# Five blocks instead of four in two query groups of a fused attention and MLP kernel, with a new instruction order

## The chip, the cores and the metric

The kernel runs on one core of one Trainium2 chip. The metric is the device time of one execution in microseconds, the median of several runs. The core has five engines: TensorE (PE, matmuls into PSUM), VectorE (DVE), ScalarE (ACT), GpSimd (POOL) and SyncE (SP, which issues the DMAs). PSUM has eight banks of 512 fp32 columns. The profile names the engines by their short names, and PEld is the weight load of TensorE.

## The reference

All tensors are bfloat16. `x` has 2048 rows of 640; there are 32 heads of 20 columns.

```python
xn = layernorm(x)
# A: attention
q, k, v = split_heads(xn @ wqkv)            # 32 heads, Dh = 20
p = softmax(q @ k.T * 20 ** -0.5)           # 2048 x 2048 for each head
s = (p @ v).merge_heads() @ wo
# B: a mixer and an MLP
h = gelu(layernorm(xn) @ w1)                # its four quarters are shifted by 1, -1, 2, -2 rows
x1 = xn + shifted(h) @ w2
g = silu(x1 + gelu(layernorm(x1) @ w3) @ w4)  # w3: 640 x 1536, w4: 1536 x 640
return x + s * g
```

Most of the work is the softmax: 32 x 2048 x 2048 exponentials.

## The kernel before

**Tiling.** Four heads make a quad, so there are eight quads (0 to 7), and each quad has four query groups of 512 queries (`qc` 0 to 3). A group is named quad_group below: 3_3 is quad 3's last, 7_1 is quad 7's second. In a group the 2048 keys are 16 key tiles of 128. A score tile is one head, one key tile and 512 queries, and takes one PSUM bank, so a group has 64 score tiles.

**Two ways to the exponential.** On the plain way (`k` in `order`, function `score_act`), TensorE makes the four score tiles of a key tile, ScalarE takes two banks at a time through Exp (L1707: 128x1024) into the buffer `PT`, and four matmuls (L1447) multiply them by V and add into the group's bank `PVB`, which is bank 7. A *wide* key tile (`w`, `score_rows`) has its four scores made in one burst, and one ScalarE instruction of 128x2048 takes all four banks (L1684).

The other way is a *block* (`b`, functions `score_both` and `block_bits`): two key tiles, eight score tiles. Four of them go to ScalarE as above (two instructions at L1707). The other four are made on VectorE: each is scaled and written as uint16 (L1729, 128x512, the names `u...`), which makes the bits of a bfloat16 power of two. To lower the error this is done with four offsets: the bits themselves, and three copies with a constant added (the "pieces" `s..._1` to `s..._3`). Each of the four versions is multiplied by V (L1629, four matmuls each). So the VectorE half of a block costs sixteen matmuls where the plain way has four.

Blocks go through `block_bits` in units of one or two. The pieces of a unit of two blocks are 4096 wide, those of a single block 2048. A piece is made on VectorE (L1617) unless the set `PP` names it by the number of the unit's first block and the offset; then GpSimd makes it (L1615, as int32). Outside group 0_0, `PP` names pieces 2 and 3 of the unit that starts with block 0 and piece 3 of the unit that starts with block 2.

`ND` says for each group how many blocks it has, and `UNITS[ND]` says after which plain key tiles they come (position, place in the unit, size of the unit):

```python
UNITS[4] = ((0, 0, 2), (1, 1, 2), (3, 0, 2), (5, 1, 2))
UNITS[5] = ((0, 0, 2), (1, 1, 2), (3, 0, 2), (4, 1, 2), (6, 0, 1))
self.BLK = [(2, 3), (6, 7), (10, 11), (14, 15), (0, 1)]
out.append(("r" if i in rows else "w" if 100 + i in rows else "k", ks[i]))   # in order(); i counts the plain key tiles
```

`NR[7][1]` is `(107,)`: in group 7_1 the plain key tile number 7 is wide, if the group has that many. A group with four blocks has eight plain key tiles (0 to 7), one with five has six (0 to 5). `NR[3][3]` is `(112,)`, which no group with four blocks reaches.

**Scores on TensorE.** The score of a head needs 20 of the 128 rows. It is made either as one matmul on 32 rows ("rows", L1638), where the matmuls of several heads that stand behind one another run at the same time on different rows, or as four matmuls of 32 columns on all rows ("columns", L1655), against queries of which only that head's rows are not zero. Which it is follows from the neighbours in TensorE's order.

**The end of a group.** `normalise` reads bank 7 with a transpose on VectorE (L1748), takes the reciprocal of the sums (L1755), multiplies on GpSimd (L1761) and sends the result to memory. The next group's first product with V can only be written after L1748.

**The rest.** All projections (L748) of the attention and of branch B are put between the scores on TensorE. Branch B needs ScalarE for its two Gelus (L2018; L2110, twice two instructions of 128x6144) and a Tanh (L2138), and VectorE for the evictions (L2103, L1314, L1376, L2012, L2046, L2132). During quad 7 the output projection of the finished groups starts, and `last_half` works on group 7_3 in two halves.

**The order.** Every engine works through a fixed list. The lists come from one string, `TABLE`: each entry is two characters for a task's number, then one character for each PSUM bank set or `PT` slot that it takes. `follow` reads it from front to back, `plan_sync` puts in the semaphore waits. So the order on each engine, the bank of every tile and the rows-or-columns choice all come from the string.

Of the kernel before, what the change touches and what calls it, by code (L numbers as in the profile page):

```python
# [490 lines left out]
class Cfg:  # L491
# [5 lines left out]
    def __init__(self, S=2048, D=640, H=32, F=1536):  # L497
# [114 lines left out]
        self.ND[6][1] = 5  # L612

# [58 lines left out]
class Gen:  # L672
# [1481 lines left out]
    r"#9###Z#0#,#%#$#[#]#6#&#:#'#w#(#^$`#)$S#d%p#5#;&R#`$'#l#<#_#=#c#b#>&Q#-#4#?#2#.$K#f#@&S#g#a#A#*#B#h$L#p#C#e#n#D#i#m$J#E#j#q#F$N$M#o#G#k#r#H$O#+#I#s#x$T$U#J$P#K#{"  # L2154
    r"#L#t#M#|#N$V#O#y#P$Q%$$#Q#}#v#R$R#S$X#z#T#u#U#~${&$W$8$|$#%%$}%&%'$q)$)$r$v#$w$x$s$l($m$(%($y$n$o$~#V$Y$$$z$Z$t#W%##X$[#Y$u$p$,$a%n%`($*%a$]$+%b$%%c$^$5&[#%g'$-"
    r"$6%h%i$_$&%d%j$.$9%k$/%8%%.&%e&]$7%/%l%0%1&^%9%))%2%:%;%*%3($2%4%5%f%6&c$%<$0%q&d&e$:%+$@&_$3%7%,%-%=&%>$D&f&j%%?&`$A&g$4&k%@$b&l%C$;%r($C$B$1&m&n&T)%s&U%A&V&W&"
    r"X#7$c&o%B%t&$<%u&Y%v&w%&a$E%m&x$?%o&y&z$>&{$d%w$F*@%&|%E*;'*<&*?$$G%x&h*=%'(%')$='*&6$$e'+$f%D$I&7*A#',*9'$g*8&'-$h&8*:)&9&}%$H&:*5%*4$$i&;$j*+&*6'**'&~(H%y'#'$"
# [136 lines left out]
```

## Time and profile before

| | |
|---|---|
| median of 3 runs | 779.2 us (778.91 to 779.86) |
| the profiled execution | 780.64 us, its span 778.9 us |
| granted TensorE clock | 0.997 |
| TensorE, ScalarE, VectorE, GpSimd busy | 767.8, 761.1, 701.4, 441.3 us |

Where the stages of the change lie is read from the transposes at L1748, one at the end of each group: group 3_3 runs from 371.6 to 404.4 us and group 7_1 from 698.5 to 720.8 us. Group 3_3 is longer than the others (20 to 24 us), because two of the Gelu instructions at L2110 stand in it.

A line of a group view reads: line, engine, operation, output <- input with shapes, xcount | busy us, mean ns of one | idle us of the engine just before them, and what ended it. Busy time counts overlapped instructions once, so the busy time divided by the count is less than the mean duration where instructions overlap. A line of the windows view gives, for a stretch of time, the busy us of each engine and in brackets how many instructions started in it.

### The profile page before, as it was taken

What the parts mean: (1) busy time and instruction counts of PE and PEld (TensorE: products, weight loads), DVE (VectorE), ACT (ScalarE), POOL (GpSimd) and SP (SyncE); (2) the same over time, 40 slices, a digit from 0 to 9 for tenths busy, and PEclk for the clock granted to TensorE, in tenths of its full rate; (3) what the DMA queues carried; (4) which work ended last, traced back from release to release, by engine and by line L of the source; (5) the groups of instructions that cost most, each with busy time, mean ns of one, the idle gap of its engine ahead of it and who ended that gap; (6) DMA issues with size and microseconds to landing.
All of it is one profiled execution on the core that took longest, in us unless ns stands there. A gap on an engine that the chain in (4) does not pass through costs nothing.

```text
span 778.9 us, 28219 instructions
## 1 busy us (share of the span) xinstructions
PE 767.8 (99%) x12594; PEld 296.5 (38%) x12594; DVE 701.4 (90%) x1177; ACT 761.1 (98%) x802; POOL 441.3 (57%) x238
## 2 busy tenths in 40 slices
PE   8999999999999999999999999999999999999996
PEld 4433333334444333233534334333334333333454
DVE  8889899988999999998988889999998899997786
ACT  7999999999999999999999999999999999999995
POOL 6386745564547657566464664766553635635742
PEclk9999999999999999999999999999999999999998
DMA  5315343364112423433343232324431023114443
GB/s 173 51 57 116 97 85 77 63 163 77 20 39 46 77 64 81 81 66 75 59 115 57 24 71 56 74 58 87 111 52 33 9 54 93 21 19 109 129 142 104
DMA packets 141353, 58.13 MB, mean 75 GB/s; under 512 B 113728, under 2 KB 136432, under 8 KB 141232
## 3 DMA queue, kind: packets, MB, share of 16 engines
q1 hardware_dynamic: 141232, 56.33, 32.8%
q8 instruction: 99, 1.62, 0.9%
q14 instruction: 22, 0.18, 0.1%
HBM read 34.70 MB, written 10.33 MB: 58 GB/s over the span
## 4 chain that ended last, share of the span: by engine, by line
PE 55%; ACT 41%; DVE 2%; DMA 1%; SPq 1%; issue 0%
ACT arena L1707 36%; PE psum L748 20%; PE psum L1638 14%; PE psum L1629 9%; PE psum L1447 7%; PE psum L1655 2%; ACT arena L2110 1%; ACT arena L1684 1%; ACT arena L2018 1%; DMA arena<-in_A_wqkv_dram 1%; SPq L935 1%; PE psum L1504 1%; ACT arena L2138 1%; PE psum L1478 1%; PE psum L1508 0%; DVE arena L1729 0%
## 5 line engine op out<-in xcount | busy, mean ns | idle before, releaser
L1707 ACT ACTIVATE arena<-psum 128x1024 bf16<-128x1024 f32 x730 | 675.0, 1075 | 5.8 <-PE psum L1638 3.7
L1615 POOL TENSOR_TENSOR arena<-arena 128x2048 int32<-128x2048 int32 x92 | 330.3, 3600 | 212.9 <-DVE arena L1617 126.3
L1729 DVE TENSOR_SCALAR arena<-psum 128x512 uint16<-128x512 f32 x532 | 342.8, 682 | 30.9 <-PE psum L1638 24.4
L748 PE MATMUL psum<-arena 128*32 128x320 bf16 (+1 forms) x5808 | 335.2, 333 | 0.4 <-ACT arena L1102 0.2
L1638 PE MATMUL psum<-arena 32*128 32x512 bf16 x1872 | 242.7, 384 | 1.4 <-ACT arena L1707 0.6
L1629 PE MATMUL psum<-arena 128*22 128x512 bf16 x2128 | 186.0, 382 | 0.2
L748 PEld LDWEIGHTS psum<-arena 128*32 128x32 bf16 x5808 | 138.2, 96 | 120.8 <-issue 44.2
L1638 PEld LDWEIGHTS psum<-arena 32*128 32x128 bf16 x1872 | 65.3, 91 | 208.9 <-ACT arena L1707 111.5
L1447 PE MATMUL psum<-arena 128*22 128x512 bf16 x1452 | 138.7, 382 | 0.0
L1617 DVE TENSOR_SCALAR arena<-arena 128x4096 uint16<-128x4096 uint16 (+1 forms) x124 | 133.7, 1095 | 1.0 <-PE psum L1629 0.2
L1629 PEld LDWEIGHTS psum<-arena 128*22 128x22 bf16 x2128 | 48.0, 90 | 63.4 <-issue 42.2
L1761 POOL TENSOR_TENSOR arena<-arena 128x512 bf16<-128x512 f32 x30 | 41.5, 1383 | 32.6 <-DVE arena L1617 27.6
L1447 PEld LDWEIGHTS psum<-arena 128*22 128x22 bf16 x1452 | 35.0, 90 | 52.0 <-issue 35.1
L1655 PE MATMUL psum<-arena 128*32 128x512 bf16 x476 | 46.3, 380 | 0.3
L2103 DVE CAST arena<-psum 128x512 bf16<-128x512 f32 x48 | 32.7, 684 | 3.8 <-PE psum L748 3.6
L1314 DVE CAST arena<-psum 128x512 bf16<-128x512 f32 x40 | 27.1, 685 | 4.7 <-PE psum L748 4.3
L1926 POOL TENSOR_TENSOR arena<-arena 128x640 bf16<-128x640 bf16 x12 | 16.8, 1402 | 21.5 <-DVE arena L1860 5.5
L959 DVE BATCH_NORM_STATS2 arena<-arena 128x6 f32<-128x320 bf16 x54 | 24.4, 477 | 1.6 <-DMA arena<-in_A_x_dram 1.6
L1748 DVE STREAM_TRANSPOSE arena<-psum 128x512 f32<-128x512 f32 x30 | 21.3, 711 | 2.5 <-PE psum L1629 1.5
L1860 DVE SCALAR_TENSOR_TENSOR arena<-psum,arena 128x320 bf16<-128x320 f32 x32 | 15.5, 486 | 8.3 <-PE psum L748 8.0
L1684 ACT ACTIVATE arena<-psum 128x2048 bf16<-128x2048 f32 x12 | 22.8, 1900 | 0.0
L2132 DVE TENSOR_TENSOR arena<-psum,arena 128x320 bf16<-128x320 f32 x32 | 15.6, 489 | 7.4 <-PE psum L748 7.2
(135 smaller groups left out, 340.9 us busy)
## 6 DMA issues: line engine op xcount, KB each, us to landing
arena<-in_B_w_dram SPq DMA_DIRECT2D x48, 160.0 KB, 2.7
arena<-arena SPq DMA_DIRECT2D x124, 32.0 KB, 1.9
arena<-in_B_w_dram SPq DMA_DIRECT2D x4, 960.0 KB, 5.5
arena<-in_A_x_dram SPq DMA_DIRECT2D x8, 320.0 KB, 5.5
arena<-in_A_x_dram SPq DMA_DIRECT2D x16, 160.0 KB, 3.0
out_dram<-arena SPq DMA_DIRECT2D x16, 160.0 KB, 2.6
heads<-arena SPq DMA_DIRECT2D x120, 20.0 KB, 2.0
arena<-keys SPq DMA_DIRECT2D x28, 80.0 KB
```

What stands on the lines that cost most here:

```text
L748: ins = e.matmul(pb[32 * c:32 * c + 32, 0:N], lhsT(k, c), rhs(k, c), start=(k == 0), stop=(stop and k == nk - 1), tile_position=(0, 32 * c))
L1447: ins = e.matmul(pb[32 * i:32 * i + 22, 0:512], VA[:, ql, kts[i // 2], i, :], PT[:, slots[i // 2][0].slot, slots[i // 2][0].at(i % 2):slot ...
L1615: return e.tensor_tensor(dst.bitcast(I32), U[:, ub, 0:w].bitcast(I32), bass.AP(c.tensor, c.offset, [list(c.ap[0]), [0, w // 2]]), op=ALU.add)
L1617: fa if onp else lambda e, v=v, dst=dst: e.tensor_scalar(dst, U[:, ub, 0:w], EXP_B[v], None, op0=ALU.add),
L1629: ins = e.matmul(pb[32 * i:32 * i + 22, 0:512], wv, dst[:, at:at + 512].bitcast(BF16), start=first, stop=final, tile_position=(0, 32 * i))
L1638: return e.matmul(out, self.KT[32 * i:32 * i + 32, b, 128 * kt:128 * kt + 128], q, start=True, stop=True, tile_position=(32 * i, 0))
L1655: ins = e.matmul(out[32 * c:32 * c + 32, :], self.KT[:, b, 128 * kt + 32 * c:128 * kt + 32 * c + 32], self.QM[:, gb, i, :], start=True, st ...
L1684: lambda e: e.activation(self.PT[:, hp[0].slot:hp[0].slot + 2, :], self.psum[:, 512 * h0.slot:512 * h0.slot + 2048].rearrange("p (a b) -> ...
L1707: lambda e: e.activation(self.PT[:, hp.slot, :].rearrange("p (a b) -> p a b", b=512), self.banks(hs), AF.Exp, scale=cfg.scale),
L1729: T("dve", c_dve(512), lambda e, h=h, y=y: e.tensor_scalar(U[:, ub, y:y + 512], self.bank(h.slot)[:, :], a_exp, EXP_BIAS, op0=ALU.mult, op ...
L1761: return e.tensor_tensor(OnT.rearrange("p (k d a) -> p a k d", k=4, a=4), Ob[:, :].rearrange("p (a k d) -> p a k d", a=4, k=4), in1, op=AL ...
L2103: T("dve", c_dve(512), lambda e, h=h, fc=fc, i=i, G=G: e.tensor_copy(G[:, i, fc, :], self.wbank(h)[:, 0:512]), reads=[wa], writes=at, name ...
```

## The change

Groups 3_3 and 7_1 get a fifth block: key tiles 0 and 1, which were plain, become the block. It is a unit by itself and comes behind the group's last plain key tile. Because 7_1 has six plain key tiles now, its number 7, the wide one, is gone. No entry of `PP` names a unit that starts with block 4. `TABLE` is replaced as a whole (16,901 characters before, 16,941 after); the new string begins with the same entries with some neighbours exchanged.

```diff
         self.ND = [list(x) for x in self.ND]
         self.ND[6][1] = 5
+        self.ND[3][3] = 5
+        self.ND[7][1] = 5
...
 TABLE = (
-    r"#9###Z#0#,#%#$#[#]#6#&#:#'#w#(#^$`#)$S#d%p#5#;&R#`$'#l#<#_#=#c#b#>&Q#-#4#?#2#.$K#f#@&S#g#a#A#*#B#h$L#p#C#e#n#D#i#m$J#E#j#q#F$N$M#o#G#k#r#H$O#+#I#s#x$T$U#J$P#K#{"
...
+    r"#9###Z#0#,#[#%#6#$#:#]#&#'#^#w#($`#d#)$S%p#;#5#`&R#<#_#=#c#>$'#l#b#-#?#4#2&Q$K#f#@#.&S#g#a#A#*#B(Q#h$L#p#C#n#e#D#i#m$J#E#j#q#F$N$T$M#o#G#k#r#H$O#+#I#s#x$U#J$P#K"
...
```

More of the change, by code (lines that the diff above doesn't have):

```diff
@@ new lines @@
+    r"V&W&X#7&o$c%B$<&Y&w$&x&y&z&{&a#8%t%%m$?%o%u$E$>%v$d%w$F*<#&|%E*@'*?&*;$$G%x&h*=#&6$&7$='((')$e$f'*%D$I'+*A(',*8#$g*9$'-$h&8(H&9&:$H&}(*4&*5'$i*:$&;$j**#*+$*6%&~"
+    r"%y'#'$'%$k*>*,)%Z$%[%F)%G%]%H'&(I%P#%Q%R%U(%V%W%^%X%S%I%z%K'%L%M%N%{&%J%Y%|%T%}%~%_*1&*C'*2%*B(%O&#*D#&&$&$&'&(&)*3'&<&**.(&+'d*-'';''<'=&%'>'?&-&H(*/&&.&I'@&p&"
+    r"2&&J'A&K&3&,&L&0*0*`'&M*_&*J#*K$*I)*H(*a$&?(*N&@&A*M'.&4'*L)&B&N&C''+''+(&&5&D*P(*Q#*O)*E+)&*T*7'/''0&=(*F*S(&q&&r*X&*W'&>*G'1'2*Y''3*[)*Z(*R%'4&s&t*U*]#&u+2&*h"
@@ new lines @@
+    r"$+3'*V&v*i%+4%*k*c(*b)'I&*l'J'K*d('L'M'N+$&+%%*^+T+&)&E*n'*o#*p$*m('5$*r'6'7*q#'8'9+5&*s+6%+*+7'':*e+C'*f#+D(*g$*v'B$(P'C+E)'D'E'F'U('V'G'W*y'X*j&'Y+<'+=&'Z+.(+"
+    r"/)+8+>('O('P+#'Q'R'S']#+:#'T+9$+X&+0''^+;%+[+W%+,)++('_'H+Z'`'a+-&*x*|+K#'b+_&+J$+`%+?+b+o'+H)+G(+1+L#+c&F)+I(*{+r+n#+U$+V%*w&G+Y'&O#,*),+(+q*z-.(J*u,,%&P,.$+v&"
+    r",-#+u%*t+y+M,/&+^'+](*}+x'f$+a('g+A$+@#,J%,K&'e'h+B#'i+|+i(+h''j,L$*~'l''k+F'c'm&i'n+j#+N3$(K+f&+e%,;#,:):V,&'o,>'p+g)+d'q+s(+t',0+w',B#,=,A&,8%,9$+k,D,<%+l)+m("
@@ new lines @@
+    r"'r#,E+O's+p)'t,@#,H&,?$,G%,#'u+P'v,I(,C#'x$'y'w'z'{'|,N%,O&,X('}+},P&,),[,x#,w$'~,W),M,Z05,y',`',Q%,R&,_(+Q,',c(M$,S(,p$,b,q#+z+R,$(N,r)(#,T,t),s(->&-?'+{,u&,e,"
+    r"F(L'[&/,5%+~-@#-1$-#(-2#,~),%-4,(-$$,d,4&-5(%##/(&(O,f,6(,v,1#,](,^),2$('((,3%,i(+((,(-(),a),z$,{#(*(.,l(/,|&,7-%((0-9'-&)-8&,h-'%-<,j(R,V#,U$-H%+S-;,Y(,}-G'-K-"
+    r"0)-/(-(,g-J-3&-M%-O#-L&-N$,o,n,k-P%-j(-R-k)(1#(Y(2-Q&1-l(-6%-7&(3($.`-U,m-:)-A(-F$-B)-E#(4(5-)-I$-X(7)(8(9(6-=-C'(:-*-h$-p#.%'-g%-i&(v(;-s-_.$(06(Z$(<([(a.&$(]-"
@@ new lines @@
+    r"x$-w#-d&-c%-D-z(=(^-e%-+-v'-{-u((_-W-y'-Y(`-}&-[-~%.1#.2$-,-T.##.5-q).('.)(-V-t-m.*)(D-Z-a%.4-`&.'-b(.8).,#.9(.+$(S#.;(T.-#(U.<-o&-n%/9)(V(W-r&/8(..(X-f/:$.=./%"
+    r".7&.6'.0$(@(>(w&.?-].:#(x-|-^(y.3&(z.B.I&-S.J(({.M$.E(?((|(A.H(B.L#)D.>.@.N&.c%.d(.T'.S&(C0I$.f.K(o--(E.U%0J.P#.g.O$.k%0K.n.Q#.D.V'.j(.W&0L.m.X(0M/k%.h$.i#0N.R("
+    r"}.A.l'/n.a(.z'.b).C.}.G)(.e#.y&.q$.p%.Y.F.|07&(F.r&/$).t(.s'/%&.Z08.u%.~$/'/#%09.o/(/&).x(.w)/F'0:/I0;.{(.v/?$0</5&/@%/6'/)/A%/+/40=&0>0?/7)0@/<%/U(/./V)/=$0A/>"
@@ new lines @@
+    r"(0C#.[450B0D0E0F/W'0G/|&/K$/{%/J#/N#0H/-/B(~$0P)#)$/}&)%0O/d$/R'/S(/1/*)&(h/T%/E#/D%/C&/;/H/0/G(/X/Y'/g/Z(/,/[%/j#)'/M&/~$0#%///P(b$0$'(c.]/](/m/^'/L&(d/_$/O/c%"
+    r"/a$/b#(e/f.^(f/e)0%0)'/i&0*((g/h%/`/l'/q/t/Q)/0R$0S0T0+$0U0&$0V0'%/2/34O'0W0X%/w0Y4R0Z0[0]48)49'4E%4F&0^0,$0-#0(4G(4</s/o/r4;4@(0.#4N'4H&4I%/z4Q/u4J&/v4C4>#4=$4"
+    r"U)4V'/y4A'4X0/4S%4T&4?(4Y/p4W%/x4L$4B4M#0_#004P)0`4j&4k%46(47)0a010b0Q4l$4]0c0e'0f4K4:#5##4r&4q%0d4`0g0h5&4s(0i5((4w'5))0j5*&4f4D4z4u&4v%4x#0k(p'4{5s(q4y#5,(4~)"
@@ new lines @@
+    r"5+'(r5%(s5-)(t4c57&56%(u4_5:'52#5/(50'51)5.55)=4b53%5I$59%._5458&5J#4^5K&5<4a4|)4}(4n'5;5H5$))>()?5B4o&4e)@4p'4g$Eg5T)4h#5S()A5?0s5'5U%4Z4[)B5>0n4i)4d)C5a)5M&5L"
+    r"'5b(5E4t)K5d5N#5X%5W$))&5e)*5[()+5Z)5Y(5P&5Q'),5]5R'5O5_%5`$5^)-5=5c&).5w&5u(5v'5t)&b5V025z4m5x#)R6K$5~#6L%5y5F5C6M%5A6%&Z6*'036+(5}&5G6$6,'5@5|)6'%6($5k5f6)$5D"
+    r"5{(5g6I'61#6H&5l5i5m6J)60%(i'645h5j6#((j63(k6/&6.'5n0468#67%6_)6^(62&(l6:6&(m6-6;6b(66%65&6O'6N(n6=69#)E$6P()F)6)G6Q%7H)H6m%6R#6S$6n&0l6>)I6T'6A6G)J0m#0o6@6o$6?"
@@ new lines @@
+    r"0p6X$6g(6f)6Y#6U6[6<6h#)o6W&6V%6])L#)M6Z&5o6j(6`$6i)6a#)N6c)O6D6k%)P6{&6d6|%6e7#))Q6B6u#6w)6t$6v(6l)v6z6y6x'7=')0(7<&)10q)27>%6p)6}$6~#6q(Ef)37%#371)479'7$7:&6C"
+    r"6r&7;)6F)573$76)72#75(6s7()Y77#)7()8)h)97?74&):7+7@&);6E7A$)S&)<7P$7.)T)U)V7Q%7T')W7'78)X7I(7J'7L)7K&7,7M&7O7R#7g$7h%7&7N7B7k#7S)8('8)(7U5p7-7)7V8*(7b&7`$7c#7a%"
+    r"7*7e708?)5q7d%7/7f8>()Z)7C7j'8@)7i#8-$8,%)})[7m)])a80$7W7l7v8/)8%(8&')^828'&7y8<$8.#8;%)_83)818='84(86'8+)`5r7n87%)b&898E%8F$85&)c88)d8G#8e'8d(8f&8K)8A8N)e)f8g%"
@@ new lines @@
+    r"7D8h$)g8L)8B&8:8i)8O8C')i&8~)j7p8D%)k8o$8n%8l)8k()l)m8p()p)7s)q)n8j)r8m$8S'8v$8u#8R%0r)s8V)t8H8I))u8J(8q8w&8M)8U7r8Q#8r&8s'8P$7q8T$)w(7E)x)y7t)z8t(7]$7{(7[#7z)7"
+    r"w8Y7F7oEt)7u){)~#*#)|7|'7^#3%*$*%*(EuEh(8]EiEj*&7xEk9-(9%#9B$9&)*'El8`Ev9E3#0tEn#Eo8_Em7GEpEwEq9)8^8Z90Ex8xEz$9(E{E|ErEyE}9,(9;$9<#9C%*)Es8bE~9?1%)1&11#1'9F121("
+    r"1)13141*3&&3H(8c9/153I7X&163'3J3(9>3K3L7Y'3)F#8a8[3*7Z$3M3;%34$353+36373893%7~#7}$399I3<?C3=3>0u$0v0w0x8#)0y3?92&0z3B#9L3C3D3@94%3E3F9$$9A(9##3G8XF%7_9S'9@)96%9"
@@ new lines @@
+    r"T&8$9'&9U(3-&3.3/0{'300|9D)318W95&9O0}8y9*'97#0~1#9+(321=$1>1$1?9.'1@1A9e&99%9:$9t#1B9K9=$8z9h989r'9q(9d)9J:W9s#17)9u$9g8{9118199R:X9v'9W(9k'9l%9V)1::Y9o9G8|9X)"
+    r"1;9b$9c#9n9P:&%1<:%)9Z(:v9['9w:)9Y9f$9]&1U):(1V9|%:-#9{$9})1W:01X:,):+(:*'9Q:/1C&:.(1Y1D9_%1Z9^$8}:19`#1E1F9x&9i)9y'9j(1G9H9m':^:31+':91,9a1H1-1.9z&1/9p10:$):#("
+    r":A#9M:_:'$:@$:>'?M&:[1b(?P1c1d:B'1e1f:=(9N1g1I$:<:?#:`:a:K$1J:61K1L:L$1M2Z#2[2]2^1N:2:C:H(:G):Z:b2_:I#:7:D%2`?G#:E&?F$::?JA%:M:F'?D)?^'?E(?I:89~?H(?a?V&?W%?N$?d"
```

183 lines of the change are left out of this document (78 added, 105 removed).

## The prediction

> **What bounds the kernel now.** I read the totals first, then the groups by form, the waits, the chain of waits, and then the stretches of the two groups that change.
>
> ```profile
> span 778.9 us, 28219 instructions
> PE 767.8 (99%) x12594; PEld 296.5 (38%) x12594; DVE 701.4 (90%) x1177; ACT 761.1 (98%) x802; POOL 441.3 (57%) x238
> PE 55%; ACT 41%; DVE 2%; DMA 1%; SPq 1%; issue 0%
> ```
>
> Two engines are full, and the chain (third line) is shared between them. The groups by form give the prices, with the rows of the operations that the change touches:
>
> ```profile
> L1707 ACT ACTIVATE arena<-psum 128x1024 bf16<-128x1024 f32 x730 | 675.0, 1075 | 5.8 <-PE psum L1638 3.7 <-PE psum L1504 1.2
> L1729 DVE TENSOR_SCALAR arena<-psum 128x512 uint16<-128x512 f32 x532 | 342.8, 682 | 30.9 <-PE psum L1638 24.4 <-PE psum L1655 1.5 <-PE psum L1629 0.7
> L1615 POOL TENSOR_TENSOR arena<-arena 128x2048 int32<-128x2048 int32 x92 | 330.3, 3600 | 212.9 <-DVE arena L1617 126.3 <-DVE arena L1729 25.1 <-DVE arena L1280 18.5
> L1629 PE MATMUL psum<-arena 128*22 128x512 bf16 x2128 | 186.0, 382 | 0.2
> L1447 PE MATMUL psum<-arena 128*22 128x512 bf16 x1452 | 138.7, 382 | 0.0
> L1638 PEld LDWEIGHTS psum<-arena 32*128 32x128 bf16 x1872 | 65.3, 91 | 208.9 <-ACT arena L1707 111.5 <-issue 43.9 <-DVE arena L1729 27.1
> L1684 ACT ACTIVATE arena<-psum 128x2048 bf16<-128x2048 f32 x12 | 22.8, 1900 | 0.0
> L1617 DVE TENSOR_SCALAR arena<-arena 128x2048 uint16<-128x2048 uint16 x33 | 22.2, 686 | 0.2 <-PE psum L1629 0.2
> ```
>
> ScalarE runs its Exps one behind the other: 675.0 us over 730 is 0.92 us each, and it idled 5.8 us before all of them together. In the other direction, the weight loads of the scores waited 111.5 us for ScalarE to free a bank. Both rows say that ScalarE sets the pace. The stretches below are group 3_3, the group behind it, 7_1 and the group behind that:
>
> ```profile
> core 0: us, PE busy (x) PEld busy (x) DVE busy (x) ACT busy (x) POOL busy (x), PEclk, DMA share, GB/s
> 371.60:404.40 32.80, 32.65 (x591) 14.61 (x588) 29.28 (x49) 32.75 (x26) 16.63 (x12) 1.00 0.39 85
> 404.40:424.40 20.00, 20.00 (x333) 7.79 (x330) 16.80 (x27) 20.00 (x22) 12.82 (x8) 1.00 0.41 80
> 698.50:720.80 22.30, 21.95 (x328) 8.39 (x330) 17.55 (x27) 22.30 (x24) 13.53 (x8) 1.00 0.37 100
> 720.80:751.10 30.30, 30.11 (x629) 15.36 (x625) 24.45 (x39) 29.46 (x32) 18.73 (x9) 1.00 0.53 145
> ```
>
> ScalarE has no idle time in the changed groups (32.75 of 32.80, 22.30 of 22.30). VectorE has some: 3.5 us in 3_3 and 3.2 behind it, 4.7 in 7_1 and 5.8 behind it. But the chain, asked for 3_3 (first line) and for 7_1 (the rest), names TensorE:
>
> ```profile
> by line: PE psum L748 51.5%; PE psum L1638 15.9%; PE psum L1655 11.2%; PE psum L1629 11.2%; PE psum L1447 8.9%; DVE arena L1314 2.1%; issue 0.2%
> ...
> by line: PE psum L1638 35.7%; PE psum L748 22.2%; PE psum L1629 18.4%; PE psum L1447 15.1%; PE psum L1655 5.2%; DVE arena L1729 3.2%; issue 0.7%
> 711.24 0.21 PE psum L1629 x4
> 711.46 0.33 PE psum L1638 x3
> 711.78 0.33 PE psum L1629 x4
> 712.11 0.98 PE psum L1638 x5
> ...
> 715.21 0.33 PE psum L1638 x4
> ```
>
> Four matmuls at L1629 cost 0.21 to 0.22 us behind other column work and 0.33 behind a burst of row scores, so a change of kind costs 0.11. A burst costs 0.33 whether it has three or four scores in it, and some bursts hold a wait (0.98). TensorE's list is thus dense as written, but how dense depends on how scores are bunched, and they are bunched worse when banks come free one by one.
>
> **The change part by part.** *ScalarE.* In 3_3 two plain key tiles (four Exps) become a block (two Exps): 2 x 0.92 = 1.85 us less. In 7_1 one plain key tile and the wide one go and two Exps come, so the narrow count stays and one wide Exp goes: 22.8/12 = 1.9. Together 3.7 us less on an engine without idle time.
>
> *TensorE.* The sixteen score tiles are made either way. In each group products with V go from two sets of four to five (one at L1447 less, four at L1629 more), so six sets of 0.22: 1.3 us more. The wide tile's four scores were one burst of 0.33 (the row at 715.21). Now they share bursts with others or make one more, 0 to 0.43 with the change of kind behind it.
>
> *VectorE.* Eight evictions at 342.8/532 = 0.64 and six pieces at 22.2/33 = 0.67 are 9.2 us, 4.6 in each group. All six pieces are VectorE's: no entry of `PP` names a unit that starts with block 4, so in spite of the words of the change GpSimd gets nothing (L1615 stays at x92). The idle time above covers 4.6 in 7_1 (4.7), and in 3_3 together with the group behind it (3.5 + 3.2). Without that cover 1.1 us would spill from 3_3. I cost it at nothing.
>
> *The end of the group.* The new block comes last in its group, so four evictions, three pieces and the transpose at L1748 stand behind one another on VectorE, and the next group's first product with V, with all that is queued behind it on TensorE, waits for the transpose. Ten groups have such a fifth block already. Here is the one that lost most, 6_1, and the sum over the ten:
>
> ```profile
> 614.90:636.20 21.30, 21.23 (x341) 7.94 (x341) 20.00 (x33) 20.50 (x24) 10.48 (x4) 1.00 0.22 49
> ...
> sum 213.80, PE 213.17 PEld 76.85 DVE 198.60 ACT 212.19 POOL 119.84; mean PE 21.32 PEld 7.68 DVE 19.86 ACT 21.22 POOL 11.98
> ```
>
> ScalarE idled 213.80 - 212.19 = 1.6 us in ten, 0.16 each, and 0.8 in 6_1. So this place costs 0.3 to 1.6 for two groups. TensorE was full in those ten (213.17 of 213.80), so a fifth block's extra sets weren't hidden in idle time there.
>
> *The new order.* The string differs from its first line on, but in neighbours. Outside the two groups it can win back at most the 5.8 us of L1707's idle time, and most of that comes from the start and the end. I take 0, with 1 us either way.
>
> *The sum.* ScalarE gives 3.7 and TensorE takes 1.3, since it stands on the chain in both groups. I charge it in full and take the end of the group as part of it: 778.9 - 3.7 + 1.3 = 776.5 for the span. The profiled execution took 780.64, 1.7 more than its span, and the median is 1.4 less than that execution, so the median becomes 779.2 - 2.4 = 776.8. The step that must hold is that bursts become fuller: 3.7 us are eight or nine bursts of 0.43 spared, and the 111.5 us of waits for ScalarE are where that could come from.
>
> **The rivals.**
>
> *TensorE is the bound, and nothing is bunched better.* For it: the chain in both groups, and TensorE full in the ten. Against it: the score loads' waits for ScalarE, and bursts like the 0.98. Then the 3.7 us become ScalarE idle time, and the run is longer by the six sets and the split wide burst: 1.3 + 0.43 = 1.7, at 781.0 (to 782 with the order's 1 us). It decides if fewer than about four bursts are spared in the two groups together. Then the ends of both show idle time on ScalarE that ended in L1638.
>
> *One group pays and the other doesn't.* 3_3 is full of projections (L748 is 51.5% of its chain) and its ScalarE time is partly Gelu, which wants no banks; 7_1 has the looser bursts. If 7_1 gives 1.9 - 0.65 and 3_3 gives nothing but its 0.65: 779.2 - 0.6 = 778.6, a time that can't be told from before.
>
> *TensorE has room, and ScalarE's whole saving shows.* For it: the waits of 111.5 us. TensorE's 1.3 would lie in them: 779.2 - 3.7 = 775.5. Against it: the chain's pieces stand behind one another with nothing between. This is what the Trainium skill would have (Perfetto Trace Analysis, Identifying the Most-Contended Engine): it calls TensorE's matmul busy time no measure and goes by the busy time of the weight loads, which is 38% on this page, so ScalarE would be the only full engine. The sets at 0.21 to 0.22 with no gap speak against that rule here, since the loads (91 ns) hide behind the streams; I give it less than the forecast.
>
> *VectorE's pieces meet GpSimd.* If a piece at L1617 must wait until a running add at L1615 is done (3600 ns), with GpSimd busy 57%, that is on average 0.57 x 1.8 = 1.0 us for each of six, an estimate from these rows: 6.2 on VectorE, whose evictions behind it hold banks. 3.7 would turn into 2.5 more: 781.7. Against it: VectorE's pieces wait for nothing (idle 0.2), it is GpSimd that waits (126.3), as the order sets the two apart. The Trainium skill (SBUF — State Buffer, Who interferes with whom) has the two engines share a port pair which the first takes for its whole instruction. The mean of 686 ns shows no such stretching of the narrow pieces.
>
> **How the numbers follow.** A measurement of this kernel can tell about 0.2% from no change, 1.6 us: faster is below 777.6, slower above 780.8. Forecast 0.33; TensorE has room 0.14 (both faster: 0.47); one group pays 0.27 (same: 0.27); TensorE is the bound 0.21; the pieces meet GpSimd 0.05 (slower: 0.26). The range goes from 775.2, the full saving with a little from the order, to 781.0, the case in which TensorE is the bound. Beyond these lie GpSimd's case, the rest of the slower one and a still faster order, under 2 in 10. As the signs are mixed: the forecast's own range is 775.8 to 777.6.
>
> **What would show it.** In the changed profile L1707 has x728, L1684 x11, L1729 x540, L1629 x2160, L1447 x1444, the 2048-wide pieces x39 and L1615 x92. If the forecast holds, ScalarE is busy about 757 us, its idle time before L1707 stays near 6, TensorE stays at 99% although it has 24 more matmuls, and the transposes behind 3_3 come about 1.2 us earlier and those behind 7_1 about 2.4. If TensorE is the bound, ScalarE's idle time before L1707 grows to 9 or more, ended by L1638. If the pieces meet GpSimd, the 2048-wide pieces get longer than 686 ns. The forecast is wrong if the transposes before 3_3 move by more than 1 us, for then the order and not the blocks decides, or if 7_1's gain is given back in the last 58 us, where the output projection waits for other things.

## The result and the profile after

The changed kernel takes 778.35 us (median; 777.65 to 779.18). The kernel before takes 779.74 beside it (778.91 to 780.56). The ratio is 0.9983, with a 95% interval of 0.9977 to 0.9989: 1.4 us, or 0.17%, faster. This lies within the 0.2% that the prediction called no change, and outside the forecast's own range (775.8 to 777.6). The profiled execution took 778.36 us.

All lines of the changed kernel behind `ND` stand two further down: L1707 became L1709, L1638 became L1640, L1655 became L1657, L748 became L750. The totals of the changed kernel and the share of each engine in the chain:

```profile
span 776.6 us, 28181 instructions
PE 765.7 (99%) x12573; PEld 294.8 (38%) x12573; DVE 708.8 (91%) x1191; ACT 758.3 (98%) x799; POOL 439.9 (57%) x238
PE 61%; ACT 36%; DVE 1%; DMA 1%; SPq 0%; issue 0%
```

TensorE took a larger part of the chain (55% before). The groups by form that the prediction named, and the column scores:

```profile
L1709 ACT ACTIVATE arena<-psum 128x1024 bf16<-128x1024 f32 x728 | 674.4, 1073 | 7.3 <-PE psum L1640 5.2 <-PE psum L1506 1.1 <-PE psum L1449 0.2
L1731 DVE TENSOR_SCALAR arena<-psum 128x512 uint16<-128x512 f32 x540 | 347.9, 682 | 28.9 <-PE psum L1640 23.9 <-PE psum L1657 0.5 <-POOL arena L1617 0.3
L1617 POOL TENSOR_TENSOR arena<-arena 128x2048 int32<-128x2048 int32 x92 | 330.1, 3599 | 219.5 <-DVE arena L1619 139.8 <-DVE arena L1731 27.9 <-PE psum L750 21.4
L1640 PE MATMUL psum<-arena 32*128 32x512 bf16 x1883 | 243.1, 384 | 2.2 <-ACT arena L1709 1.3 <-ACT arena L1686 0.3 <-DVE arena L1731 0.2
L1631 PE MATMUL psum<-arena 128*22 128x512 bf16 x2160 | 190.7, 381 | 0.0
L1449 PE MATMUL psum<-arena 128*22 128x512 bf16 x1444 | 138.2, 382 | 0.2
L1640 PEld LDWEIGHTS psum<-arena 32*128 32x128 bf16 x1883 | 65.1, 91 | 211.6 <-ACT arena L1709 113.2 <-issue 43.0 <-DVE arena L1731 30.5
L1657 PE MATMUL psum<-arena 128*32 128x512 bf16 x432 | 42.2, 381 | 0.5 <-ACT arena L1709 0.2 <-DVE arena L2014 0.2
L1619 DVE TENSOR_SCALAR arena<-arena 128x2048 uint16<-128x2048 uint16 x39 | 26.2, 686 | 0.6 <-PE psum L1631 0.5
L1686 ACT ACTIVATE arena<-psum 128x2048 bf16<-128x2048 f32 x11 | 21.1, 1919 | 0.0
```

The same view of the kernel before has one row that the prediction didn't show, the column scores:

```profile
L1655 PE MATMUL psum<-arena 128*32 128x512 bf16 x476 | 46.3, 380 | 0.3
```

The edit did what the diff says, in every count. What the prediction gave no number for are the scores: 476 column matmuls became 432, and the row scores went from 1872 to 1883. Eleven scores changed from columns (four matmuls) to rows. The balance hides two opposite moves. The table gives how far the end of a group (its transpose) shifted against the kernel before, in us; e3, e5 and e6 are experiments below:

| shift at the end of | 3_0 | 3_1 | 3_3 | 4_0 | 6_2 | 6_3 | 7_0 | 7_1 | 7_2 | last instruction |
|---|---|---|---|---|---|---|---|---|---|---|
| after | -0.16 | -0.80 | -1.70 | -1.21 | -1.55 | -2.21 | -1.00 | -0.05 | -0.23 | -2.28 |
| e3, order alone | -0.51 | -0.07 | +0.11 | +0.11 | +0.10 | +0.11 | +0.10 | +0.10 | +0.12 | -0.85 |
| e5, block of 3_3 alone | -0.41 | -1.04 | -1.95 | -1.46 | -1.62 | -1.61 | -1.62 | -1.62 | -1.70 | -2.68 |
| e6, block of 7_1 alone | -0.20 | -0.20 | -0.20 | -0.20 | -0.38 | -1.04 | +0.17 | +1.12 | +0.94 | -0.74 |

Shifts within a line are to be compared, not those of two lines, since runs of one list differ by a constant few tenths from the start. In the last column, about 1.0 us is the profiled execution of before alone: its output still ran for 3.2 us behind VectorE's last instruction (775.70 of 778.91), against 2.2 in the changed kernel (774.40 of 776.63). e3, with the same list as before from 3_1 on, shows the same 0.97 (+0.12 to -0.85). So the changed kernel wins 1.05 us from 3_0 to 4_0 and 0.35 more up to 6_2, loses 1.3 from 6_2 to 7_2, and gets 1.1 of that back at the end. The loss does not stand in 7_1 alone: 6_3 is 0.66 shorter than before, 7_0 1.21 longer and 7_1 0.95 longer.

The windows view over these stages, of before and then of after (us of the stage, then busy us and, in brackets, instructions). The edges are the ends of the transposes behind 3_0, 4_0, 6_2 and 7_2. The view also counts instructions that only reach over an edge.

```profile
core 0: us, PE busy (x) PEld busy (x) DVE busy (x) ACT busy (x) POOL busy (x), PEclk, DMA share, GB/s
328.72:425.12 96.40, 95.98 (x1536) 36.32 (x1533) 86.41 (x147) 96.35 (x94) 54.81 (x30) 1.00 0.36 76
656.87:751.85 94.98, 94.02 (x1623) 39.53 (x1620) 81.67 (x124) 94.14 (x100) 56.37 (x25) 1.00 0.32 80
751.85:778.91 27.06, 20.25 (x588) 13.85 (x580) 19.10 (x39) 18.49 (x20) 9.26 (x7) 0.92 0.34 106
```

```profile
328.57:423.92 95.35, 94.95 (x1509) 35.74 (x1503) 89.26 (x151) 95.00 (x92) 53.26 (x28) 1.00 0.33 68
655.32:751.62 96.30, 95.14 (x1673) 40.52 (x1675) 85.64 (x133) 94.25 (x100) 57.06 (x25) 1.00 0.29 73
751.62:776.63 25.01, 19.14 (x552) 12.52 (x540) 18.31 (x38) 17.54 (x19) 8.39 (x6) 0.98 0.39 130
```

From 3_1 to 4_0 TensorE has 27 matmuls fewer on record, although the block brought twelve more. From 6_3 to 7_2 it has 50 more. The first two stages for the column scores alone (first before, then after), where the second busy column is now PEld:

```profile
328.72:425.12 96.40, 12.10 (x124) 3.26 (x124) 1.00 0.36 76
656.87:751.85 94.98, 5.87 (x60) 1.58 (x60) 1.00 0.32 80
```

```profile
328.57:423.92 95.35, 6.64 (x68) 1.77 (x68) 1.00 0.33 68
655.32:751.62 96.30, 7.83 (x80) 2.11 (x80) 1.00 0.29 73
```

Around 3_3, 56 column matmuls went (14 scores); around 7_1, 20 came (5 scores). The projections hardly moved: 732 in the first stage before and after, 776 and 772 in the second, 252 and 252 behind 7_2. What moved over the end of 7_2 is work of the last group, 7_3, whose halves have matmuls of 256 columns. Here are its V-products in the last two stages (L1478 before, L1480 after):

```profile
656.87:751.85 94.98, 1.36 (x24) 0.61 (x24) 1.00 0.32 80
751.85:778.91 27.06, 6.40 (x152) 3.71 (x152) 0.92 0.34 106
```

```profile
655.32:751.62 96.30, 2.56 (x44) 1.12 (x44) 1.00 0.29 73
751.62:776.63 25.01, 5.57 (x136) 3.02 (x132) 0.98 0.39 130
```

With them eight of its row scores (L1504) moved ahead, 44 to 52, and behind 7_2 they went from 52 to 48 and its column scores (L1508) from 96 to 80.

With the prediction's prices TensorE's list can be added up. Four matmuls of 512 columns take 0.216 us, so a column matmul is worth 0.054; a burst of row scores takes 0.33; a set of V-products 0.22. The matmuls of 7_3 are read from three lines of the chain of before:

```profile
756.42 1.09 PE psum L1478 x36
759.71 0.34 PE psum L1504 x8
752.09 0.44 PE psum L1508 x16
```

That is 0.030, 0.043 and 0.028 each. Bursts, counted in the traces, went from 66 to 68 around 3_3 and from 66 to 62 from 6_3 to 7_2.

| | columns | bursts | V-product sets | work of 7_3 | sum | measured |
|---|---|---|---|---|---|---|
| 3_1 to 4_0 | -56 x 0.054 = -3.0 | +0.7 | +0.65 | 0 | -1.7 | -1.05 |
| 6_3 to 7_2 | +20 x 0.054 = +1.1 | -1.3 | +0.65 | +20 x 0.030 + 8 x 0.043 = +0.95 | +1.4 | +1.3 |
| behind 7_2 | 0 | 0 | 0 | -16 x 0.030 - 4 x 0.043 - 16 x 0.028 = -1.1 | -1.1 | -1.1 |

The sign of each stage comes out, and the size within 0.7 us; one price for every burst is rough, as the burst of 0.98 among the prediction's lines shows. The sum says where the time of TensorE went, and no more: TensorE is busy for 99% of the first two stages in both kernels, so its list and their length must change together. It isn't shown by it that a shorter list on TensorE alone would shorten a stage.

By the prediction's prices ScalarE's saving was nearly the same in both places (1.85 and 1.9). Of its busy time 1.35 us went in the first stage. In the second it rose by 0.1. One narrow Exp more stands in it, and behind a wait an Exp overlaps with none before it: in the trace of the changed kernel one by itself took 1.05 us and two in a row 1.94.

### The profile page after: what moved, and what is told of

It reads as the page before. It is cut to its first block, busy times and chain, and to the rows that moved or that the text cites. A ratio compares the mean times of both kernels' runs of the same rounds, so it can differ in the third digit from the quotient of the medians.

```text
span 776.6 us, 28181 instructions
## 1 busy us (share of the span) xinstructions
PE 765.7 (99%) x12573; PEld 294.8 (38%) x12573; DVE 708.8 (91%) x1191; ACT 758.3 (98%) x799; POOL 439.9 (57%) x238
## 3 DMA queue, kind: packets, MB, share of 16 engines
q8 instruction: 98, 1.61, 0.8%
## 4 chain that ended last, share of the span: by engine, by line
PE 61%; ACT 36%; DVE 1%; DMA 1%; SPq 0%; issue 0%
ACT arena L1709 31%; PE psum L750 23%; PE psum L1640 16%; PE psum L1631 10%; PE psum L1449 7%; PE psum L1657 2%; ACT arena L2112 1%; ACT arena L2020 1%; ACT arena L2140 1%; DMA arena<-in_A_x_dram 1%; ACT arena L1686 1%; PE psum L1506 1%; PE psum L1480 1%; PE psum L1510 0%; ACT L1709 0%; DVE arena L1885 0%
## 5 line engine op out<-in xcount | busy, mean ns | idle before, releaser
L1709 ACT ACTIVATE arena<-psum 128x1024 bf16<-128x1024 f32 x728 | 674.4, 1073 | 7.3 <-PE psum L1640 5.2
L1617 POOL TENSOR_TENSOR arena<-arena 128x2048 int32<-128x2048 int32 x92 | 330.1, 3599 | 219.5 <-DVE arena L1619 139.8
L1731 DVE TENSOR_SCALAR arena<-psum 128x512 uint16<-128x512 f32 x540 | 347.9, 682 | 28.9 <-PE psum L1640 23.9
L750 PE MATMUL psum<-arena 128*32 128x320 bf16 (+1 forms) x5808 | 338.6, 333 | 0.3 <-ACT arena L1104 0.2
L1640 PE MATMUL psum<-arena 32*128 32x512 bf16 x1883 | 243.1, 384 | 2.2 <-ACT arena L1709 1.3
L1631 PE MATMUL psum<-arena 128*22 128x512 bf16 x2160 | 190.7, 381 | 0.0
L750 PEld LDWEIGHTS psum<-arena 128*32 128x32 bf16 x5808 | 137.3, 96 | 123.3 <-issue 49.3
L1640 PEld LDWEIGHTS psum<-arena 32*128 32x128 bf16 x1883 | 65.1, 91 | 211.6 <-ACT arena L1709 113.2
L1619 DVE TENSOR_SCALAR arena<-arena 128x4096 uint16<-128x4096 uint16 (+1 forms) x130 | 137.9, 1078 | 1.7 <-PE psum L1631 1.1
L1449 PE MATMUL psum<-arena 128*22 128x512 bf16 x1444 | 138.2, 382 | 0.2
L1631 PEld LDWEIGHTS psum<-arena 128*22 128x22 bf16 x2160 | 49.4, 90 | 60.2 <-issue 40.8
L1657 PE MATMUL psum<-arena 128*32 128x512 bf16 x432 | 42.2, 381 | 0.5 <-ACT arena L1709 0.2
L978 POOL TENSOR_SCALAR arena<-arena 128x640 bf16<-128x640 bf16 x16 | 13.9, 876 | 18.8 <-DVE arena L1619 15.7
L1686 ACT ACTIVATE arena<-psum 128x2048 bf16<-128x2048 f32 x11 | 21.1, 1919 | 0.0
```

What stands on the lines that cost most here:

```text
L750: ins = e.matmul(pb[32 * c:32 * c + 32, 0:N], lhsT(k, c), rhs(k, c), start=(k == 0), stop=(stop and k == nk - 1), tile_position=(0, 32 * c))
L1449: ins = e.matmul(pb[32 * i:32 * i + 22, 0:512], VA[:, ql, kts[i // 2], i, :], PT[:, slots[i // 2][0].slot, slots[i // 2][0].at(i % 2):slot ...
L1617: return e.tensor_tensor(dst.bitcast(I32), U[:, ub, 0:w].bitcast(I32), bass.AP(c.tensor, c.offset, [list(c.ap[0]), [0, w // 2]]), op=ALU.add)
L1619: fa if onp else lambda e, v=v, dst=dst: e.tensor_scalar(dst, U[:, ub, 0:w], EXP_B[v], None, op0=ALU.add),
L1631: ins = e.matmul(pb[32 * i:32 * i + 22, 0:512], wv, dst[:, at:at + 512].bitcast(BF16), start=first, stop=final, tile_position=(0, 32 * i))
L1640: return e.matmul(out, self.KT[32 * i:32 * i + 32, b, 128 * kt:128 * kt + 128], q, start=True, stop=True, tile_position=(32 * i, 0))
```

## The experiments

The edits are given against the changed kernel, with "..." where code is left out.

**e3: the order without the blocks.** The new string up to 3_1, the old one from there on, and no new block.

```diff
-        self.ND[3][3] = 5
-        self.ND[7][1] = 5
...
 TABLE = ( # the new string to 3_1, then the old one
```

> The changed kernel's list up to group 3_1, the list of before from there; no block is added. Theories A and B: 0 to 0.3 us below before, as the transposes up to 3_1 stand 0.1 to 0.4 us earlier in the changed profile. Theory C: 1 us or more below before.

Measured: 780.12 us, ratio 0.9999 (0.9990 to 1.0008). The neighbours exchanged ahead of 3_1 give nothing that shows: the shift of the changed kernel is -0.16 at the end of 0_0 and still -0.16 at that of 3_0. But e3 has a join too, and it lost 0.6 us there (-0.51 at 3_0, +0.11 behind 3_1), so its time isn't that of the order alone. What the order does from 3_1 on goes with the block and isn't tried here.

**e1 and e2: one block each, joined in 6_3.** e1 has the new string to the middle of 6_3 and the old one behind it, e2 the other way round.

```diff
-        self.ND[7][1] = 5   # e1; e2 takes out ND[3][3] = 5 instead
...
 TABLE = ( # joined in 6_3
```

> The changed kernel's list up to the middle of group 6_3, the list of before from there: the fifth block in 3_3 stays, the one in 7_1 is undone. Theory A (the block in 3_3 pays, the one in 7_1 gives its ScalarE time back as idle time in 7_1 and 7_2): the whole gain stays, 1.2 to 1.5 us below before, ratio 0.998. Theory B (each block pays the same): half of it, 0.7 us, ratio 0.999. Theory C (the new order pays, not the blocks): some part that has nothing to do with 3_3; the transposes in 3_1 and before would already stand 1 us earlier.

> The list of before up to the middle of group 6_3, the changed one from there: only 7_1 has its fifth block. Theory A: no gain, within 0.3 us of before, with 1 to 2 us of ScalarE idle time in 7_2. Theory B: 0.7 us below before. The rival that TensorE is the bound in 7_1, without anything to make up for the extra products: 0.6 us above before.

Measured: 781.44 us for both, ratios 1.0019 (1.0010 to 1.0029) and 1.0018 (1.0009 to 1.0026). They tell nothing about the blocks. e1 ran with the changed kernel to 6_1 and then lost 3.1 us against the kernel before up to the end of 6_3 (-1.36 to +1.77), at the join itself. The stretch around it, first in the changed kernel and then in e1:

```profile
650.00:674.00 24.00, 24.00 (x387) 8.96 (x379) 21.68 (x34) 24.00 (x27) 15.87 (x6) 1.00 0.17 30
```

```profile
650.00:674.00 24.00, 22.56 (x322) 7.63 (x319) 20.03 (x31) 22.16 (x25) 12.06 (x4) 1.00 0.10 18
```

Both engines idled there, while both are busy for all of the 24 us in the two lists by themselves. A list that is cut where tasks are in flight costs more than the change in question.

**e5 and e6: one block each, joined where the two lists agree.** The join lies in 6_2, and the `PT` slots behind it are renamed so that they match.

```diff
-        self.ND[7][1] = 5   # e5; e6 takes out ND[3][3] = 5 instead
...
 TABLE = ( # joined in 6_2, slots renamed
```

> As e1 (3_3 with its fifth block, 7_1 without), but the two lists are joined at a place in group 6_2 where both hold the same banks, and the PT slots are renamed to fit, so that nothing waits at the join (e1 lost about 3 us there). Theory A (the block in 3_3 pays, the one in 7_1 does not): 1.2 to 1.5 us below before, ratio 0.998. Theory B (each pays half): 0.7 us below.

> As e2 (only 7_1 has its fifth block), joined at the same place without a wait. Theory A: within 0.4 us of before. Theory B: 0.7 us below. TensorE as the bound in 7_1 with nothing to make up: 0.6 us above.

Measured: e5 778.41 us, ratio 0.9978 (0.9968 to 0.9989); e6 779.89, ratio 1.0001 (0.9992 to 1.0010). The whole gain comes from the list up to 6_2, with 3_3's block; what follows gives nothing. In e6 the groups 6_3 to 7_2 lose 1.3 us, as they do in the changed kernel, and the end gives about half of it back. Where ScalarE's saving in 7_1 went is seen in 7_2, the group behind it, here in e5 and then in e6:

```profile
719.89:750.15 30.26, 30.06 (x632) 15.42 (x625) 24.38 (x39) 29.51 (x32) 18.53 (x10) 1.00 0.54 146
```

```profile
722.62:752.79 30.17, 30.11 (x649) 15.85 (x652) 26.19 (x44) 28.21 (x30) 19.64 (x10) 1.00 0.44 119
```

With the block ScalarE idles 1.96 of 30.17 us there and 0.75 of 30.26 without, and TensorE is full in both (0.06 and 0.20 idle). The list of waits names what it waits for, in the changed kernel in 7_2:

```profile
ACT arena L1709 <- PE psum L1640: 1.7, 4, 0.5
```

Four waits for row scores make 1.7 us (one of 0.6 before).

**e4 and e11: without the repeated scores in 7_2.** Three score matmuls of 7_2 are made twice in both lists; e4 takes the repeats out of the changed kernel, e11 out of e5.

```diff
-..., (6, 3, 14, 3): 1, (7, 2, 2, 3): 1, (7, 2, 3, 1): 2}
+..., (6, 3, 14, 3): 1}
```

> The changed kernel without the three repeated score matmuls that group 7_2 has in both kernels (they write the same scores again). If TensorE is the bound in 7_2 (theory A), up to 3 x 0.21 = 0.6 us below the changed kernel, 2.0 below before, less if they run beside another head's score. If ScalarE is the bound there, no difference from the changed kernel.

> The version of e5 (fifth block in 3_3 alone), without the three repeated score matmuls of group 7_2. It should beat both kernels: 1.7 us below before from e5, and 0.1 to 0.4 more if TensorE is the bound from 7_2 to the end (e4 gained 0.2 in that stage), so 2.0 below before, ratio 0.9975. If the repeats ran in ScalarE's shadow, as e5: 0.998.

Measured: e4 778.52 us, ratio 0.9974 (0.9964 to 0.9984); e11 778.23, 0.9979 (0.9969 to 0.9988). Neither can be told from the kernel that it was taken from. In e4's trace the end stands 0.20 earlier against the changed kernel than the groups ahead of 7_1 do (+0.61 to +0.41). e11 beats the kernel before; that it beats the changed one is not shown. Its expectation, 0.1 to 0.4 us more than e5, missed: against e5 its trace is level at the end of 7_2, within 0.03 us, and 0.4 later at the end.

**e7, e9 and e12: less for TensorE alone.** Nine sets of V-products in 7_1 (e7), 3_3 (e9) or 7_2 (e12) stream 32 columns instead of 512, so most of these products is left out. Nothing else is changed. The added line moves those behind it by one: L1631 is L1632 here, L1640 L1641, L1709 L1710.

```diff
-    ins = e.matmul(pb[32 * i:32 * i + 22, 0:512], wv, dst[:, at:at + 512].bitcast(BF16),
+    n_ = 32 if (quad, qc) == (7, 1) and v and j < 3 else 512   # e9: (3, 3), e12: (7, 2)
+    ins = e.matmul(pb[32 * i:32 * i + 22, 0:n_], wv, dst[:, at:at + n_].bitcast(BF16),
```

> The changed kernel; in 7_1 the products with V of offsets 1 to 3 of blocks 0 to 2 (nine sets of four matmuls) stream 32 columns and not 512, so the rest of these products is left out: up to 9 x 0.2 = 1.8 us less on TensorE, nothing else. If TensorE is the bound in 7_1 and 7_2 (theory A), the end comes 0.8 to 1.8 us earlier than the changed kernel's. If ScalarE is the bound there, no difference.

> The changed kernel; in 3_3 the products with V of offsets 1 to 3 of blocks 0 to 2 (nine sets) stream 32 columns and not 512, so the rest of these products is left out: up to 1.8 us less on TensorE. If TensorE is the bound in 3_3, as the chain before showed it, the transposes behind 3_3 come 1 to 1.8 us earlier than in the changed kernel. If ScalarE is, less than 0.4 us.

> The changed kernel; in 7_2 the products with V of offsets 1 to 3 of blocks 0 to 2 (nine sets) stream 32 columns and not 512, so the rest of these products is left out: up to 1.8 us less on TensorE, as in e7, but one group later. If TensorE is the bound from the start of 7_2 on, the end comes 1.2 to 1.8 us earlier than the changed kernel's (e7 gained nothing). If something else is (ScalarE, the transfers of the output), less than 0.4 us.

First, the relief was smaller than a whole set. In the timeline of e7 (start, us) a short set is followed by the next burst:

```profile
708.78 0.19 PE L1632 MATMUL psum<-arena 128*22 128x32 bf16 x4
708.90 0.96 PE L1641 MATMUL psum<-arena 32*128 32x512 bf16 x5
```

It holds TensorE 0.12 us where a full one holds it 0.22, so nine relieve it by about 0.9.

Measured: 778.32 us (ratio 0.9975, 0.9965 to 0.9985), 778.17 (0.9977, 0.9968 to 0.9986) and 778.39 (0.9979, 0.9970 to 0.9988). In the traces, against the changed kernel and without the constant from the start, e7 gains 0.0 us, e9 0.15 to 0.2 and e12 0.1. Most of the relief became idle time of TensorE. First the changed kernel around 3_3, 7_1 and 7_2, then e9 around 3_3, e7 around 7_1 and e12 around 7_2:

```profile
372.00:404.00 32.00, 32.00 (x588) 14.61 (x584) 29.97 (x51) 31.95 (x25) 17.41 (x12) 1.00 0.25 66
700.00:720.00 20.00, 19.62 (x310) 7.60 (x306) 16.50 (x24) 19.91 (x23) 9.87 (x6) 1.00 0.43 119
720.00:752.00 32.00, 31.95 (x701) 16.88 (x693) 27.82 (x46) 30.04 (x31) 20.18 (x10) 1.00 0.45 118
```

```profile
372.00:404.00 32.00, 31.68 (x590) 14.18 (x586) 30.15 (x52) 31.95 (x26) 18.15 (x12) 1.00 0.29 67
```

```profile
700.00:720.00 20.00, 18.82 (x312) 7.44 (x306) 16.40 (x24) 19.91 (x23) 9.56 (x6) 1.00 0.45 126
```

```profile
720.00:752.00 32.00, 31.11 (x701) 16.57 (x697) 27.73 (x46) 29.93 (x32) 20.20 (x10) 1.00 0.46 118
```

In 7_1 and 7_2 TensorE idles 0.8 us more, in 3_3 0.3. The waits of TensorE, in 7_1 of e7 and in 7_2 of e12, show for whom:

```profile
PE psum L1641 <- ACT arena L1710: 0.7, 3, 0.4
PE psum L1449 <- ACT arena L1710: 0.2, 1, 0.2
PE psum L1658 <- ACT arena L1710: 0.2, 1, 0.2
```

```profile
PE psum L1506 <- ACT arena L1687: 0.5, 1, 0.5
PE psum L1449 <- ACT arena L1710: 0.2, 1, 0.2
```

All three speak against TensorE as the only bound, which was to show as a gain of 0.8 us or more. In 7_1 ScalarE is full as well (19.91 of 20). In 7_2 it has room, and still e12 won only 0.1. The gaps of ScalarE in e12 lie between 727.9 and 740.3 us, while five of the nine short sets run behind 745; the 0.5 us wait for a wide Exp stands right behind four of them, at 746.7. This reads as if the two engines took turns at being late within one group, so that relief at one place is lost at the next place where the other engine is behind.

**e8 and e10: less for ScalarE alone.** Five Exps of 7_1 (e8) or 3_3 (e10) take 256 of the 512 columns of each bank and leave out the rest, about 2 us less work.

```diff
+    lambda e, n_=256 if tag in ('7_1_4_0', '7_1_4_1', '7_1_5_0', '7_1_8_0', '7_1_8_1') else 512: ...   # e10: 3_3_...
```

> The changed kernel; in 7_1 five Exps take 256 of the 512 columns of each bank, the other half of their output is left out: 5 x 0.43 = 2.1 us less on ScalarE, nothing else. If TensorE is the bound in 7_1 and 7_2 (theory A), less than 0.4 us earlier than the changed kernel. If ScalarE is the bound, 1.5 to 2.1 us earlier.

> The changed kernel; in 3_3 five Exps take 256 of the 512 columns of each bank, the other half of their output is left out: 2.1 us less on ScalarE. If ScalarE is the bound in 3_3, the transposes behind it come 1.5 to 2.1 us earlier than in the changed kernel. If TensorE is, less than 0.4 us.

Measured: 778.02 us (0.9973, 0.9963 to 0.9983) and 778.35 (0.9978, 0.9969 to 0.9987). In the traces e8 gains 0.2 up to 7_1 and 0.34 to the end, e10 nothing: all its group ends from 3_1 to 7_2 shift by the same +0.03 (behind 7_2, where its list is again that of the changed kernel, it ended 0.3 later). ScalarE's share of it, e8 around 7_1 and e10 around 3_3:

```profile
700.00:720.00 20.00, 19.72 (x314) 7.69 (x310) 16.44 (x25) 18.66 (x23) 9.69 (x6) 1.00 0.45 124
```

```profile
372.00:404.00 32.00, 32.00 (x588) 14.56 (x584) 30.00 (x51) 30.62 (x25) 17.38 (x12) 1.00 0.28 66
```

ScalarE idles 1.3 us more in each (19.91 to 18.66, 31.95 to 30.62) and TensorE stays where it was. A saving on ScalarE alone, as large as the one that a block brings, is worth 0 to 0.3 us in these lists.

## Why the prediction was right, and where it was not

The forecast was 2.4 us less than before, and 1.4 were measured; 778.35 lies in the whole range, though not in the forecast's own, and the direction was right. That the number came as near is partly luck: one of the two groups paid and the other didn't, where the forecast had both pay.

*ScalarE's 3.7.* The counts came as said (x728, x11). The busy time fell by 2.8, to 758.3 and not to about 757, and idle time before L1709 rose from 5.8 to 7.3, between the 6 of the forecast and the 9 of its rival. That the whole saving counts was the weak step: e8 and e10 took about 2 us more from it, and 0 to 0.3 arrived.

*The block of 3_3.* The step gave 1.85 - 0.65 = 1.2, and "about 1.2 us earlier" behind 3_3; measured were 1.55 at the end of 3_3 and 1.05 at that of 4_0 (0.75 to 1.6 at the next three), and e5 shows that this is the whole gain. The size was right, the account was not. It rested on ScalarE setting the pace with 0.65 charged for TensorE, but TensorE's busy time fell by 1.0 us in this stage instead of rising, since 14 scores were made as rows and no longer as columns. So both full engines had less to do here. The step that the forecast called the one that must hold, fuller bursts, held in another form: no burst was spared, 14 more row scores took two more bursts. And the waits of the score loads for ScalarE, from which it was to come, stayed: 111.5 us before, 113.2 after.

*The block of 7_1.* This is the step that failed. It gave 1.9 - 0.65, and 2.4 us earlier behind 7_1; measured was -0.05 there, and e6 is at 1.0001. From 6_3 to 7_2 there were four bursts fewer, but five scores had gone from them to columns, three sets were added, and 0.95 us of 7_3's work moved ahead; TensorE's busy time rose by 1.1 us. ScalarE's saving turned into its waits at L1640. The end gave 1.1 of the lost 1.3 back. The term of 1.25 measured about 0: by the medians nothing can be told, and in the traces the block with its order costs 0.14 us (the changed kernel against e5, from 3_0 to VectorE's last instruction) or 0.45 (e6 against before), where the end alone can vary by 0.3 (e10).

*TensorE's sets at 1.3.* The count was right (x2160, x1444). What was left out was larger: the choice between rows and columns moved 56 matmuls one way (3.0 us by the price above) and 20 the other (1.1).

*VectorE at nothing.* Right: eight evictions made 5.1 us (347.9 - 342.8) and six pieces 4.0 (26.2 - 22.2), and ScalarE's list of waits names no VectorE instruction. The pieces still take 686 ns and GpSimd's 3599, so the rival in which they meet is out; so is the stretching that the Trainium skill's shared port (SBUF — State Buffer, Who interferes with whom) would have made possible.

*The order at 0, give or take 1.* Right as far as 3_0, where the shift is that of 0_0. The sign named for it, a transpose ahead of 3_3 that moves by more than 1 us, came and can't be read as meant: the end of 3_2 is 6 us later, as the first of the two Gelu instructions at L2110, which still begins near 375 us (376.43 before, 374.88 after), now stands in 3_2 and no longer in 3_3. But 0.65 of the 1.05 us stand at the end of 3_1 already, two groups ahead of the block. Work moved between these groups, so this alone doesn't say whose it is; behind 3_0, order and block were only tried together.

*The rivals.* "One group pays and the other doesn't" came true in kind, and its 778.6 is 0.25 from the result, but with the groups exchanged: it gave 7_1 the gain for its loose bursts and 3_3 none. "TensorE is the bound" was right that ScalarE's saving in 7_1 becomes idle time that ends in L1640. It was wrong that TensorE alone sets the time there, as e7 took 0.9 us from it for nothing, and that nothing is bunched better: the scores of 3_3 were. "TensorE has room" is out. The rule of the Trainium skill behind it (Perfetto Trace Analysis, Identifying the Most-Contended Engine) judges TensorE by its share of the peak rate and by the busy time of the weight loads, and the latter is again at 38%. By it the saving of ScalarE should have shown in full, at 775.5, and e10 should have gained about 2 us more; the measurements decide against it here.

*The last 58 us.* The warning was half right: 7_1's gain was gone before them, and they lost nothing. Behind 7_2 1.1 us came back, since V-products and scores of 7_3 had been done already and four of its scores went from columns to rows.

What fits all runs is that a stage gets shorter by more than 0.35 us only where both full engines have less to do: around 3_3 both had, from 6_3 to 7_2 ScalarE alone was to have less, and in e7 to e10 and e12 one of them alone had. This is worked out; no run took work from both at one place. Open too is how much of 3_3's gain is the block's and how much the 14 scores that its order moved to rows. No run had the one without the other.

## What to carry to other kernels

Where two engines are both full and hand buffers to each other in fixed lists, a saving on one of them may be none of time, as here: ask what the same edit does to the other engine's list in the same stage, and count all of it, with the work whose form follows from the order (here scores as columns or rows). Add up both lists by stage, by the counts of the windows view, before the price of the edit itself. And when two lists are joined for an experiment, join them where they agree, for a bad join cost 3 us here and hid an effect of 1.

## What the runs showed of the hardware

Runs of the same list repeat closely: between the changed kernel and e10, all group ends from 3_1 to 7_2 differ by 0.03 us, and others by a constant of up to 0.6 from the start. So effects of 0.1 to 0.2 us can be read from traces up to 7_2 where medians, with intervals of 0.5 to 0.8 us each way, can't show them. Behind 7_2 that doesn't hold: e10 ended 0.3 later there without a change, and the output of before took 1.0 longer than that of the changed kernel. A matmul set cut from 512 to 32 columns still held TensorE for 0.12 us instead of 0.22.
